# Retention recurrence on quarters of the TensorE array in 256-token steps, with a new order of the first steps

## The chip, the cores and the metric

The kernel runs on one core of a Trainium2 chip. The metric is the time of one execution on the device in microseconds (us). The kernel before takes 194.77 us, the median of three runs (194.75 to 195.33).

A core has a matrix engine, TensorE (PE in the profile; its weight loads, which overlap its matmuls, are PEld), and three others that are used here: VectorE (DVE), ScalarE (ACT) and GpSimd (POOL). SyncE's queue (SP) issues all DMAs. PE multiplies a stationary operand (`lhsT`, loaded as weights) with a moving one (`rhs`) and writes to PSUM, which has eight banks of 512 float32 a partition; DVE and ACT read PSUM, POOL only SBUF.

## What is computed

```python
gamma = 1.0 - 2.0 ** (-5.0 - np.arange(H))          # H = 8 heads, D = 64, S = 768, B = 4
for t in range(S):
    state = gamma * state + einsum('bhd,bhe->bhde', k[:, :, t], v[:, :, t])
    y[:, :, t] = scale * einsum('bhd,bhde->bhe', q[:, :, t], state)
x = y.transpose(0, 2, 1, 3).reshape(B * S, H * D)     # 3072 x 512
out = ((x @ w1) * (x @ w2)) @ w3 @ w_out              # 512 -> 1024 -> 1024 -> 512
```

The first half is a linear attention whose state (64 x 64 a head) decays by a factor of its head. The second is an FFN with a product of two projections. Inputs and output are float32; matmuls run in float16.

## The kernel before, in words

**Weights.** `w3 @ w_out` is multiplied out once: the rows of w3 are cast to float16 (`cast_w3`), transposed on PE (`w3_transpose`, lines 270 and 279), copied back (line 262) and multiplied with w_out (lines 291 and 304) to `W3O`. The FFN then has three products for each block of tokens: `a_unit` (w1) and `b_unit` (w2) through `mm`, line 537, eight blocks each, and `o_unit` (line 563) for each 128 tokens. ACT copies a's PSUM to SBUF (line 547), DVE multiplies b's PSUM into it (line 553), ACT scales and copies the output (line 568), and SP stores it (line 570).

**Recurrence.** It goes in chunks of 128 tokens, 24 in all, six to a sequence. For a chunk:

- `scores` (line 466): k times q, eight matmuls of 128x128x128. Two heads share the 128 partitions, so k is padded with zeros: `kp` holds the one head's k in partitions 0 to 63 and zeros below, and the other way round for the other head. DVE multiplies the result with the causal mask `keep` (line 471).
- `outputs`: v times the masked scores (lines 506 and 507; `vp` is padded in the same way) and, but for the first chunk of a sequence, the state times q (line 509). DVE scales with `YS` and writes x transposed, `xt` (line 514).
- `kv` (line 489): k times v. DVE adds the old state (line 497), POOL multiplies with the decay `GS`, whose zeros keep the two heads apart (line 498).

The decay within a chunk is in two exponentials, one multiplied into v (`VS`, POOL, line 383, which is also the cast of v), one into the output (`YS`). q and k are cast by POOL (lines 338 and 379) and transposed: in the first chunks on PE (lines 359, 400, 450), later by DMA (lines 420 and 424). ACT copies the transposed k into its padded place (lines 440 and 441).

**Order.** The Tile framework sets the semaphores, and each engine runs its instructions in program order. The opening is written out by hand (lines 674 to 812): w3 in column and row pieces as they land, chunks 0 to 3, and the FFN of the first 256 tokens by rows of the weights (`by_rows`, line 760). Then `step(n)` runs for each chunk (line 631): `fill` is a queue of FFN units with estimated costs, and `fill.pull` places them between scores, state and outputs, so that PE has work while DVE and POOL do theirs. `load_chunk(n + 4)` and `casts(n + 2)` run ahead.

Of the kernel before, what the change touches and what calls it, by code (L numbers as in the profile page):

```python
# [10 lines left out]
HP = mybir.dt.float16  # L11
AF = mybir.ActivationFunctionType
MULT = mybir.AluOpType.mult
ADD = mybir.AluOpType.add
PSUM = bass.MemoryType.PSUM
# [3 lines left out]
def kernel(  # L19
# [13 lines left out]
    C = 128  # L33
    WST = 12
    NCH = S // C
    NSTEP = B * NCH
    NTOK = B * S
    DT0 = 6
    NP = H // 2
    DM = 512  # L40
    DFF = 1024

# [5 lines left out]
    wstage = ctx.enter_context(tc.tile_pool(name="wstage", bufs=WST))  # L48
    xpool = ctx.enter_context(tc.tile_pool(name="xpool", bufs=4))
    ld = ctx.enter_context(tc.tile_pool(name="ld", bufs=6))  # L50
    att = ctx.enter_context(tc.tile_pool(name="att", bufs=2))
    fsb = ctx.enter_context(tc.tile_pool(name="fsb", bufs=2))

    ps_t = ctx.enter_context(tc.tile_pool(name="ps_t", bufs=1, space=PSUM))
    ps_at = ctx.enter_context(tc.tile_pool(name="ps_at", bufs=1, space=PSUM))
    ps_f = ctx.enter_context(tc.tile_pool(name="ps_f", bufs=3, space=PSUM))
# [4 lines left out]
    def dma_in(dst, src):  # L61
        nc.sync.dma_start(dst, src)  # L62

    chunk_in = {}
    q_in = {}
    pair_in = {}

    def load_pair(m, names="qkv"):

        b, c = divmod(2 * m, NCH)  # L70
        for nm, src in (("q", q), ("k", k), ("v", v)):
            if nm not in names:
                continue
            if nm == "q":
                t = ld.tile([128, 2 * 512], FP, tag="q64", name="q64", bufs=3)
                q_in[m] = t
            else:
                t = new_stage()
                pair_in[nm, m] = t
            dma_in(  # L80
                t[:, :].rearrange("p (h x) -> p h x", x=2 * D),
                src[b, :, c * C : (c + 2) * C, :].rearrange("h (p t) d -> p h (t d)", t=2),
            )

    def load_q4(half):

        t = ld.tile([128, 2 * 512], FP, tag="q64", name="q256", bufs=3)
        dma_in(
            t[:, :].rearrange("p (h x) -> p h x", x=4 * D),
            q[0, half * 4 : half * 4 + 4, 0 : 4 * C, :].rearrange("h (p t) d -> p h (t d)", t=4),  # L90
        )
        q_in["half", half] = t

    def load_chunk(n):
        if n >= NSTEP:
            return
        b, c = divmod(n, NCH)
        tiles = []
        if c % 2 == 0:

            t = ld.tile([128, 2 * 512], FP, tag="q64", name="q64", bufs=3)
            dma_in(
                t[:, :].rearrange("p (h x) -> p h x", x=2 * D),
                q[b, :, c * C : (c + 2) * C, :].rearrange("h (p t) d -> p h (t d)", t=2),
            )
            q_in[n // 2] = t
        for nm, src in (("k", k), ("v", v)):
            t = ld.tile([128, 512], FP, tag=nm + "32", name=nm + "32")
            dma_in(
                t[:, :].rearrange("p (h d) -> p h d", d=D),  # L110
                src[b, :, c * C : (c + 1) * C, :].rearrange("h i d -> i h d"),
            )
            tiles.append(t)
        chunk_in[n] = tiles

    def new_stage():
        return wstage.tile([128, 1024], FP, tag="wst", name="stg")

    def load_rows(src, i):
        t = new_stage()  # L120
        dma_in(t[:, :], src[i * 128 : (i + 1) * 128, :])
        return t

    def load_wo(i):

        t = new_stage()
        dma_in(
            t[:, :].rearrange("p (t n) -> p t n", t=2),
            moe_w_out[i * 256 : (i + 1) * 256, :].rearrange("(p t) n -> p t n", t=2),
        )  # L130
        return t

    def load_w3_columns(i):

        t = new_stage()
        dma_in(
            t[:, :].rearrange("p (f c) -> p f c", f=4),
            moe_w3[0:512, i * 256 : (i + 1) * 256].rearrange("(f p) c -> p f c", p=128),
        )
        return t  # L140

    w3c_st, wo_st = [], []
    for i in range(4):
        w3c_st.append(load_w3_columns(i))
        wo_st.append(load_wo(i))
    w3_st = {f: load_rows(moe_w3, f) for f in range(4, 8)}
    load_q4(0)
    load_q4(1)
    load_pair(0, "kv")
    w1_st = [load_rows(moe_w1, d) for d in range(4)]  # L150
    load_pair(1, "k")
    w2_st = [load_rows(moe_w2, 0)]
    load_pair(1, "v")
    w2_st += [load_rows(moe_w2, d) for d in range(1, 4)]
    for n in range(4, 8):
        load_chunk(n)
# [3 lines left out]
    KP = [const.tile([128, NP, 2, 128], HP, name=f"kp{i}") for i in range(2)]  # L160
    VP = [const.tile([128, NP, 2, 128], HP, name=f"vp{i}") for i in range(3)]

    def zero(t):
        nc.vector.memset(t[:, :, :, :].rearrange("p a b c -> p (a b c)").bitcast(FP), 0.0)

    zero(VP[0])
    ident16 = const.tile([128, 128], HP, name="ident16")
    make_identity(nc, ident16[:, :])


    ip_i = const.tile([128, H], mybir.dt.int32, name="ip_i")
    nc.gpsimd.iota(ip_i[:, :], pattern=[[0, H]], base=1, channel_multiplier=1)
    if_i = const.tile([128, 128], mybir.dt.int32, name="if_i")
    nc.gpsimd.iota(if_i[:, :], pattern=[[1, 2], [2, 64]], base=1, channel_multiplier=0)
    LGH = const.tile([128, H], FP, name="LGH")
    LGP = const.tile([128, NP], FP, name="LGP")
    for h in range(H):
        r = (h % 2) * 64
        nc.gpsimd.memset(LGH[:, h : h + 1], -math.log(gam[h]))
        nc.gpsimd.memset(LGP[r : r + 64, h // 2 : h // 2 + 1], math.log(gam[h]))  # L180

    keep = const.tile([128, 128], FP, name="keep")
    nc.gpsimd.memset(keep[:, :], 1.0)
    nc.gpsimd.affine_select(
        out=keep[:, :], in_=keep[:, :], compare_op=mybir.AluOpType.is_ge, fill=0.0,
        base=0, pattern=[[1, 2], [2, 64]], channel_multiplier=-1,
    )


    VS = const.tile([128, H], FP, name="VS")  # L190
    YS = const.tile([128, NP, 128], FP, name="YS")
    GS = const.tile([128, NP, 128], FP, name="GS")
    vs_x = const.tile([128, H], FP, name="vs_x")
    nc.vector.tensor_tensor(vs_x[:, :], ip_i[:, :], LGH[:, :], MULT)
    if_f = const.tile([128, 128], FP, name="if_f")
    nc.vector.tensor_copy(if_f[:, :], if_i[:, :])
    nc.scalar.activation(VS[:, :], vs_x[:, :], AF.Exp)
    for p in range(NP):
        nc.scalar.activation(YS[:, p, :], if_f[:, :], AF.Exp, scale=LGP[:, p : p + 1])

    keep2 = const.tile([128, 128], FP, name="keep2")
    nc.gpsimd.memset(keep2[:, :], 1.0)
    for t in range(2):
        r = slice(t * 64, t * 64 + 64)
        nc.gpsimd.affine_select(
            out=keep2[r, :], in_=keep2[r, :], compare_op=mybir.AluOpType.is_ge, fill=0.0,
            base=-t, pattern=[[1, 2], [2, 64]], channel_multiplier=-2,
        )

    ip2_i = const.tile([128, 2, H], mybir.dt.int32, name="ip2_i")  # L210
    for c in range(2):
        nc.gpsimd.iota(
            ip2_i[c * 64 : c * 64 + 64, :, :], pattern=[[1, 2], [0, H]], base=1, channel_multiplier=2
        )

    zero(KP[0])
    zero(KP[1])

    for i in (1, 2):
        nc.gpsimd.memset(VP[i][:, :, :, :].rearrange("p a b c -> p (a b c)").bitcast(FP), 0.0)  # L220
    nc.gpsimd.memset(GS[:, :, :], 0.0)
    for h in range(H):
        p, r = h // 2, (h % 2) * 64
        nc.gpsimd.memset(GS[r : r + 64, p, r : r + 64], gam[h] ** C)

    XT = {}


# [5 lines left out]
    W3h = {}  # L234
    w3t = {}

    def cast_to(dst, src, on_dve):
        if on_dve:
            nc.vector.tensor_copy(dst, src)  # L239
        else:  # L240
            nc.scalar.copy(dst, src)  # L241

    def cast_wo(i):
        cast_to(WO[i][:, :, :].rearrange("p a n -> p (a n)"), wo_st[i][:, :], i % 2 == 1)

    def cast_w3(key, st):
        t = att.tile([128, 1024], HP, tag="w3h", name="w3h", bufs=4)
        cast_to(t[:, :], st[:, :], False)
        W3h[key] = t
# [3 lines left out]
    def bank(tag, shape, dtype, name):  # L253
        return (ps_t if tag == "psT" else ps_at).tile(shape, dtype, tag=tag, name=name)

    def w3_bank(key, i):
        src, tag = W3h.pop(key), ("psA1", "psK")[i % 2]
        return src, ps_at.tile([128, 1024], HP, tag=tag, name="psW3")

    def w3_back(key, ps):  # L260
        t = att.tile([128, 1024], HP, tag="w3t", name="w3t", bufs=3)
        nc.vector.tensor_copy(t[:, :], ps[:, :])  # L262
        w3t[key] = t
# [601 lines left out]
```

## Time and profile before

| | before |
|---|---|
| median of three runs | 194.77 us |
| span of the profiled execution, first to last instruction | 193.1 us |
| what the timed runs have around the span | 1.7 us |
| first matmul starts, last one ends | 1.5 us, 190.1 us |
| PE busy | 184.1 us (95%) |
| DVE, ACT, POOL busy | 117.0, 103.3, 83.6 us |
| matmuls | 1785 |
| DMA | 40.5 MB, 84007 packets |

The profile is of one execution. "Busy" is the time in which an engine had an instruction in it; matmuls overlap, so a busy PE says only that it did not stand empty. "The chain that ended last" is followed back from the last instruction, at each step to what released it. Clock: PE was granted its full clock throughout.

### The profile page before, as it was taken

The numbers are of one execution on the slowest core, as the hardware profiler recorded it, in microseconds if no ns is written. First come the engines' busy times: TensorE is split into PE (matmuls) and PEld (weight loads), VectorE is DVE, ScalarE is ACT, GpSimd is POOL, SyncE is SP. The second block draws the span as 40 slices with busy tenths as digits, with TensorE's granted clock in tenths as the row PEclk, the third lists the DMA queues.
The fourth block names the chain that finished last, engine by engine and source line by source line (L and its number), as shares of the span: only waits on it lengthen the run. The fifth ranks groups of instructions, "written<-read, shape, count | busy, mean of one in ns | idle before, by whom it ended". The sixth has DMA issues, their size and how long they took to land.

```text
span 193.1 us, 4713 instructions
## 1 busy us (share of the span) xinstructions
PE 184.1 (95%) x1785; PEld 139.8 (72%) x1785; DVE 117.0 (61%) x220; ACT 103.3 (54%) x198; POOL 83.6 (43%) x144
## 2 busy tenths in 40 slices
PE   6698999979999999999999999999999999999993
PEld 2234557778797789777977797788777877887752
DVE  3225479699587758656665676565656665753220
ACT  6478598972454465354635463555355545533322
POOL 7600257728864737476252742863426432200000
PEclk9999999999999999999999999999999999999999
DMA  6999999998999999999999989969979930111104
GB/s 207 349 389 398 326 377 355 368 266 198 235 204 221 199 231 237 144 247 211 231 273 187 223 188 223 206 149 270 199 178 201 206 94 19 59 54 54 38 28 154
DMA packets 84007, 40.54 MB, mean 210 GB/s; under 512 B 61329, under 2 KB 78993, under 8 KB 83985
## 3 DMA queue, kind: packets, MB, share of 16 engines
q1 hardware_dynamic: 83984, 40.25, 88.5%
q8 instruction: 14, 0.23, 0.5%
q14 instruction: 9, 0.07, 0.2%
HBM read 29.36 MB, written 6.29 MB: 185 GB/s over the span
## 4 chain that ended last, share of the span: by engine, by line
PE 81%; DMA 10%; ACT 4%; DVE 2%; SPq 1%; issue 0%
PE psF L537 39%; PE psO L563 21%; DMA q<-in_q_dram 6%; PE psA L466 5%; DMA stg<-in_moe_w_out_dram 5%; PE psY L506 3%; PE psY L507 3%; PE psF L760 2%; PE psY L509 2%; PE psK L489 2%; SPq L62 1%; PE psG L537 1%; PE psO L580 1%; ACT w3o L241 1%; PE psG L760 1%; DVE vp L329 1%
## 5 line engine op out<-in xcount | busy, mean ns | idle before, releaser
L537 PE MATMUL psF<-xt,w 128*128 128x256 f16 (+1 forms) x736 | 85.0, 266 | 0.0
L537 PEld LDWEIGHTS <-w 128*128 128x128 f16 x768 | 68.2, 98 | 7.2
L553 DVE TENSOR_TENSOR ht<-pa,psF 128x256 f16<-128x256 f32 x88 | 36.6, 416 | 22.4 <-PE psF L537 13.1
L547 ACT COPY pa<-psF 128x256 f32<-128x256 f32 x84 | 31.3, 372 | 33.4 <-PE psF L537 33.0
L471 DVE TENSOR_TENSOR am<-psA,keep 128x512 f16<-128x512 f32 x48 | 30.9, 684 | 21.4 <-PE psA L466 21.3
L563 PE MATMUL psO<-w3o,ht 128*128 128x512 f16 x184 | 43.3, 379 | 0.0
L498 POOL TENSOR_TENSOR t<-s,GS 128x512 f16<-128x512 f32 x15 | 19.3, 1285 | 38.7 <-DVE s L497 38.7
L568 ACT ACTIVATE osb<-psO 128x512 f32<-128x512 f32 x23 | 13.7, 598 | 37.3 <-PE psO L563 37.3
L563 PEld LDWEIGHTS <-ht 128*128 128x128 f16 x184 | 17.8, 98 | 16.9 <-DVE ht L806 0.2
L383 POOL TENSOR_TENSOR vp<-v,VS 128x256 f16<-128x256 f32 x40 | 23.8, 617 | 6.9 <-DMA v<-in_v_dram 3.3
L514 DVE TENSOR_TENSOR xt<-psY,YS 128x512 f16<-128x512 f32 x24 | 17.8, 742 | 4.1 <-PE psY L509 3.8
L506 PE MATMUL psY<-am,vp 128*128 128x128 f16 x96 | 16.8, 219 | 0.9 <-POOL vp L329 0.7
L507 PE MATMUL psY<-am,vp 128*128 128x128 f16 x96 | 16.7, 219 | 0.6 <-DVE vp L329 0.6
L466 PEld LDWEIGHTS <-kp 128*128 128x128 f16 x192 | 12.5, 98 | 4.5 <-DVE kp L239 0.2
L338 POOL CAST q<-q 128x1024 f16<-128x1024 f32 x10 | 10.6, 1057 | 11.9 <-DMA q<-in_q_dram 11.9
L379 POOL CAST k<-k 128x512 f16<-128x512 f32 x20 | 12.3, 613 | 5.5 <-DMA v<-in_v_dram 2.4
L497 DVE TENSOR_TENSOR s<-psK,t 128x512 f32<-128x512 f32 x16 | 11.0, 688 | 2.8 <-PE psK L489 2.5
L262 DVE COPY w3t<-psW 128x1024 f16<-128x1024 f16 x8 | 5.5, 690 | 10.9 <-PE psW L270 8.5
L466 PE MATMUL psA<-qTd,kp 128*128 128x128 f16 x144 | 11.1, 219 | 0.0
L509 PE MATMUL psY<-qTd,t 128*128 128x128 f16 x60 | 10.8, 219 | 0.0
L440 ACT COPY kp<-kT 64x512 f16<-64x512 f16 x17 | 10.5, 618 | 0.4
L441 ACT COPY kp<-kT 64x512 f16<-64x512 f16 x17 | 10.5, 615 | 0.4
(87 smaller groups left out, 193.9 us busy)
## 6 DMA issues: line engine op xcount, KB each, us to landing
stg<-in_moe_w_dram SPq DMA_DIRECT2D x16, 512.0 KB, 8.5
q<-in_q_dram SPq DMA_DIRECT2D x12, 512.0 KB, 5.4
out_dram<-osb SPq DMA_DIRECT2D x23, 256.0 KB, 3.2
k<-in_k_dram SPq DMA_DIRECT2D x20, 256.0 KB, 5.3
v<-in_v_dram SPq DMA_DIRECT2D x20, 256.0 KB, 5.5
stg<-in_moe_w_out_dram SPq DMA_DIRECT2D x4, 512.0 KB, 8.2
stg<-in_k_dram SPq DMA_DIRECT2D x2, 512.0 KB, 9.9
stg<-in_v_dram SPq DMA_DIRECT2D x2, 512.0 KB, 9.7
```

The source lines that it names most:

```text
L383: nc.gpsimd.tensor_tensor(vp[:, :, r, r * 64 : r * 64 + 64], v32[:, :].rearrange("j (p s e) -> j p s e", s=2, e=64)[:, :, r, :], VS[:, :]. ...
L466: nc.tensor.matmul(ps[:, i, r, :], lhsT=kp[:, p, r, :], rhs=queries(n, p), start=True, stop=True)
L471: nc.vector.tensor_tensor(am[:, half * 2 : half * 2 + 2, :, :].rearrange("j p s i -> j (p s) i"), ps[:, :, :, :].rearrange("j p s i -> j ( ...
L498: eng.tensor_tensor(t16[:, :, :], s32[:, :, :], GS[:, :, :], MULT)
L506: nc.tensor.matmul(ps[:, p, :], lhsT=vp[:, p, 0, :], rhs=am[:, p, 0, :], start=True, stop=False)
L507: nc.tensor.matmul(ps[:, p, :], lhsT=vp[:, p, 1, :], rhs=am[:, p, 1, :], start=False, stop=(c == 0))
L509: nc.tensor.matmul(ps[:, p, :], lhsT=Tst[0][:, p, :], rhs=queries(n, p), start=False, stop=True)
L514: nc.vector.tensor_tensor(XT[n // 2][:, :, n % 2 * C : (n % 2 + 1) * C].rearrange("p a (i t) -> p a t i", t=2), ps[:, :, :].rearrange(orde ...
L537: nc.tensor.matmul(ps[:, i * w : (i + 1) * w], lhsT=W[d][:, (f + i) * 128 : (f + i + 1) * 128], rhs=XT[self.tok0 // TB][:, d, c0 : c0 + w] ...
L547: nc.scalar.copy(self.pa[f][:, :], ps[:, :])
L553: nc.vector.tensor_tensor(self.HT[:, f : f + TB // self.width, :].rearrange("p f n -> p (f n)"), self.pa.pop(f)[:, :], ps[:, :], MULT,)
L563: nc.tensor.matmul(psO[:, :], lhsT=self.HT[:, f, tb * 128 : (tb + 1) * 128], rhs=W3O[f][:, :], start=(f == 0), stop=(f == 7),)
```

## The change

The FFN and the product of w3 and w_out compute what they did, in the same matmuls. What is different:

- **Steps of 256 tokens** (`T`), 12 in all, three to a sequence, in place of chunks of 128. Loads, casts and transposes are by step.
- **Quarters.** Each matmul of the recurrence takes 64 partitions and gives 64: its `lhsT` and `rhs` lie in one half of the partitions, its result in one half, so that it stands on one quarter of the array. Nothing is padded with zeros any more: `KP`, `VP`, and ACT's copies into them are gone, as is the 128-wide `GS`. `QUARTERS` is the order in which the four are issued.
- **Chunks of 64 tokens from step 2 on** (`EO = 2`); steps 0 and 1 keep chunks of 128, with even and odd tokens in turn. Scores and av are then done for 64 x 64 blocks, and there are four states a step (`state`, three DVE sums and one that POOL decays).
- **`fence`**: ACT copies one column of each chunk from the PSUM of `inter` (state times q) to a tile that nothing reads, before `av` adds into the same PSUM.
- **Order.** A step's scores, k'v, masks and states are computed one step ahead, its casts three ahead and its transposes two. On PE each step is `inter(n)`, `scores(n + 1)`, `kv(n + 1)`, `av(n)`, the two output units of step n - 1, and the a- and b-units of step n, two blocks of 256 columns to a PSUM bank, so that ACT and DVE read 512 columns at a time. `fill` and its costs are gone.
- **The opening** is a new list: loads (w3 in rows alone, k of step 0 before the last of them, w1 and w2 by rows in another order), which engine casts what, and the place of every piece, until step 4. The warm-up has 8 matmuls of 512 columns, not 13.

The core of the diff follows: the quarters; the matmuls of scores from step 2 on, of k'v (`o` is `KB[n][g][half(r), t, a, :]` there), of `inter`, then `fence`, and `av`; the order of the loads; and the main loop (`LAST` is 3):

```diff
+    QUARTERS = ((0, 0), (1, 1), (0, 1), (1, 0))
+    def half(x):
+        return slice(x * 64, x * 64 + 64)
+    def qchunk(n, r, a, s, g):
+        c = 2 * s + g
+        return qT[n][half(r), :, a, c * 32 : (c + 1) * 32]
...
+            ps = [bank(t, [128, NP, 2, 64]) for t in tags]
+            for a in range(NP):
+                for s in range(2):
+                    for r, g in QUARTERS:
+                        nc.tensor.matmul(
+                            ps[r][half(g), a, s, :], lhsT=kT[n][half(r), s, a, half(g)],
+                            rhs=qchunk(n, r, a, s, g), start=True, stop=True,
+                        )
...
+                    nc.tensor.matmul(
+                        o, lhsT=k16[n][half(g), t, hd], rhs=v16[n][half(g), t, hd],
+                        start=(a == 0 and t == 0), stop=(t == 1), skip_group_check=True,
+                    )
...
+                        o, rhs = X[n, g][half(r), a, s * 64 : (s + 1) * 64], qchunk(n, r, a, s, g)
+                    nc.tensor.matmul(
+                        o, lhsT=TS[n, c][half(r), a, :], rhs=rhs, start=((g, r) not in begun), stop=False,
+                        skip_group_check=True,
+                    )
...
+    def fence(n):
+        for g in range(2):
+            if (g, 0) in X[n]:
+                s0 = 0 if n < EO or (n, (0, g)) in TS else 1
+                t = att.tile([128, NP, 2 - s0], FP, tag=f"fence{g}", name="fence")
+                nc.scalar.copy(t[:, :, :], X[n, g][:, :, :].rearrange("p a (s i) -> p a s i", s=2)[:, :, s0:, 0])
...
+                        o, rhs = X[n, g][half(r), a, t * 64 : (t + 1) * 64], am[n, None, r][half(g), a, t, :]
+                    nc.tensor.matmul(
+                        o, lhsT=v16[n][half(g), t, h * D : (h + 1) * D], rhs=rhs,
+                        start=((g, r) not in begun), stop=(n >= EO or t == 1), skip_group_check=True,
+                    )
...
+    fetch(
+        "r4 wo0 r1 r2 wo1 r5 wo2 r3 r6 k0 r7 wo3 q0 v0 r0 q1 k1 v1 w11 w13 w10 w12 w22 w23 w21 w20 "
+        "v2 v3 k2 q2 k3 v4 q4"
+    )
...
+    for n in range(LAST, NS):
+        nxt = n + 1 < NS
+        if n > LAST:
+            inter(n, ("X0", "X1"))
+            fence(n)
+            if nxt:
+                scores(n + 1, ("S0", "S1"))
+                kv(n + 1, ("K", "F1"))
+            av(n)
+            x_out(n, 0)
+            x_out(n, 1)
+            if nxt:
+                states(n + 1)
+                mask(n + 1, 0)
+                mask(n + 1, 1)
...
+            loads(n + 4)
+            casts(n + 3)
+            o_unit(n - 1, 0, ("F2",))
+            o_out(n - 1, 0)
+            o_unit(n - 1, 1, ("F0",))
+            o_out(n - 1, 1)
+        tags = ("F2", "F0", "F1")
+        for u in range(4):
+            a_unit(n, u, tags[2 * u % 3])
+            b_unit(n, u, tags[(2 * u + 1) % 3])
+            if n == LAST:
+                catch_up(u)
+        if n > LAST:
+            cast_queries(n + 3)
```

In the load list rN, woN, w1N and w2N are pieces of 512 KB of w3, w_out, w1 and w2, and kN, qN, vN are step N's. The list of the opening's pieces (some 190 lines) runs from the warm-up to the a- and b-blocks of steps 0 and 1, done by rows of w1 and w2 as these land, and to steps 2 and 3, whose recurrence is broken into shorter pieces between output units. In it `o_unit(0, 0)` is the first output unit.

## The prediction

> **What bounds the kernel now.** I read the page's engine table and slices first, then the chain that ended last, then one period of that chain, then the DMA share by stage.
>
> ```profile
> span 193.1 us, 4713 instructions
> ...
> PE 184.1 (95%) x1785; PEld 139.8 (72%) x1785; DVE 117.0 (61%) x220; ACT 103.3 (54%) x198; POOL 83.6 (43%) x144
> ...
> PE   6698999979999999999999999999999999999993
> ...
> PE 81%; DMA 10%; ACT 4%; DVE 2%; SPq 1%; issue 0%
> ```
>
> TensorE (PE) has no free slice from the middle of the span on, and the chain is PE for 81%; the DMA and ACT shares are the opening. The chain between 104.7 and 117.9 us holds one period of 256 tokens (start, length, what):
>
> ```profile
> 104.73 0.45 PE psA L466 x8
> 105.17 1.31 PE psF L537 x12
> 106.48 0.22 PE psK L489 x4
> ...
> 109.56 1.73 PE psO L563 x8
> ...
> 117.85 0.06 PE psA L466
> ```
>
> PE waits for nothing here. The paces are 0.45/8 = 56 ns for 128 columns, 1.31/12 = 109 ns for 256 and 1.73/8 = 216 ns for 512, so a matmul with its weight load costs its columns. The period is 117.85 - 104.73 = 13.12 us. The FFN takes 64 x 109 + 16 x 216 ns = 10.44 of it (lines 537 and 563). The recurrence takes the other 2.68: scores 2 x 0.45, state 2 x 0.22, outputs 2 x 12 x 56 ns = 1.34.
>
> By the groups of PE's instructions kept apart by shape, there are 820 matmuls of 128 columns, 688 of 256, 261 of 512, and 16 of the last output. At these paces (136 and 83 ns for the last 16, in proportion to their columns) that is 179.0 us. PE's last matmul ends at 190.1, so 11 us are lost, nearly all before 46.8 us, where the output matmuls of the first 256 tokens start. So two things can gain: fewer PE cycles in the recurrence, and a denser opening.
>
> **The recurrence, steps 2 to 11.** A step has 256 tokens. Its 48 matmuls of 128 columns become 128 of 64 columns, each on a quarter of the array: 32 scores, 32 k'v, 32 state-times-q, 32 av (some fewer in steps that begin or end a sequence). The trace has no matmul on a quarter, so I bound its cost by the 56 ns row:
>
> - Cheapest: four run side by side, each for 64 columns, so 28 ns a group of four. The state-times-q matmuls use only the two diagonal quarters, so 28 ns a pair. 24 x 28 + 16 x 28 ns = 1.12 us a step.
> - Dearest: side by side not at all, and the number of instructions counts as now: 128 x 56 ns = 7.2 us. If columns count, 128 x 28 ns = 3.6 us.
>
> I take a value near the cheap end, 28 to 50 ns a group (1.1 to 2.0 us): the row shows a cost that follows the columns, with no floor of its own down to 128, and the four quarters have different rows, columns and PSUM halves.
>
> Going from whole-array matmuls to quarters and back may cost the overlap that the pipeline has now. A 128-column matmul lasts 219 ns (line 466) and the next starts after 56, so between 0 and 163 ns a switch; I take 163. Two switches a step in the main loop: 0.33 us.
>
> The Trainium skill ("TensorEngine Tiling (Array Packing)", Key Properties) says the same of a change of tiling mode, that it drains the engine; no run here shows it yet. A rule that speaks against the change stands in "TensorE: Matmul & The Clock Gate" (Part 1): matmuls never start closer than about 25 ns, however few their columns. By that a step would be 128 x 25 ns + 0.33 = 3.5 us and the whole about 199.6; but its Part 3 has matmuls in different tiles of the array start some 4 ns apart. The trace, with nothing under 56 ns, decides neither.
>
> **A wait is added:** `fence`. ScalarE reads the PSUM of state-times-q before `av` may add to it, so `av` waits for ACT, and behind `av` on PE stand both output units. ACT's smallest rows are 216 ns (128x16) and 331 ns (128x192), so two fences are 0.43 to 0.66; I take 0.5. Ahead of them ACT has the copy of the last a-block (0.58, line 241's 128x512) and the q cast (1.05). From the end of that last a-block on PE: ACT is free at 0.2 + 0.58 + 1.05 = 1.83. PE does the b-block (0.87), drains (0.16) and does state-times-q (0.45 to 0.8), whose result is there at 1.65 to 2.0. Fences end at 2.35 to 2.5, and PE, which has scores and k'v of the next step as cover (0.45 to 0.8), starts `av` at 2.45 to 2.65, takes 0.22 to 0.4, and drains. The stretch is 1.97 to 2.35 us. **I take 2.1 us a step against 2.68.** Without cast and fence in the way it would be 1.12 + 0.33 = 1.45.
>
> The other engines have room in a step of 10.44 + 2.1 = 12.5 us. DVE: two x_out 0.74, four states 0.42, two masks 0.68, four b-blocks 0.68 = 7.2. ACT: four a-blocks 0.58, two output copies 0.60, q cast 1.05, fences 0.5 = 5.1 (the padding copies of lines 440 and 441, 21 us in all, go). POOL: k cast 1.05, v twice line 498's 1.29, last state 0.6 = 4.2. Masks, states, casts and transposes are all done a step ahead, under FFN matmuls; without that cover masks and states alone would cost 3 us a step.
>
> **DMA** carries the same bytes in the same packet sizes. Its share by stage (us, PE, PEld, DVE, ACT and POOL busy, PEclk, DMA share, GB/s):
>
> ```profile
> 20.00:30.00 10.00, 9.57 (x86) 5.79 (x84) 6.54 (x14) 7.85 (x14) 4.76 (x7) 1.00 1.11 355
> 117.85:130.97 13.12, 13.12 (x131) 10.51 (x129) 8.44 (x16) 6.64 (x14) 6.94 (x9) 1.00 0.95 200
> ```
>
> 0.95 x 13.12 = 12.5 us of DMA a step by its own share, which counts overlapping packets, so 12.5 is an upper end. A step of 12.5 us is just at it; that is the cover most easily lost. On SP each step issues two transposes, loads and two stores; the stores wait for ACT's output copies as now (line 570), with loads for four steps on ahead of them.
>
> **The opening.** The same 26 tiles of 512 KB (13.6 MB) must land before steps 0 and 1 can finish. The first eight slices (4.83 us each) move 207 + 349 + 389 + 398 + 326 + 377 + 355 + 368 GB/s = 13.4 MB, so the last tile of w2 lands near 39 us in any order. After it the list holds a cast (0.73) and 13 groups of four 256-column matmuls (13 x 0.436 = 5.7), so steps 0 and 1 finish their a- and b-blocks at about 46. PE's own work agrees: warm-up until 5.1 (now 13 matmuls, then 8), w3 times w_out 64 x 216 + 64 x 56 ns = 17.4, q and k transposes 1.8, recurrence of two steps 2.9 (32 groups of four and 12 pairs at 56 ns, 16 groups at 28), 14 switches 2.3, a- and b-blocks 14.0: 43.5 with no wait, and 2.5 us of waits in it is my choice. Engine queues in it: DVE takes the first w3 cast (0.73, line 239) that ACT does now (1.04 from 4.59 on), behind the exponents' arguments, which wait as now for POOL's sixteen small memsets (1.4 us); what is behind it is PE's first transpose (5.68 now), so this start can move by some 0.3 us either way. k of step 0 comes 10th, q and v 13th and 14th, all before the last rows of w3, so scores can fill the waits for w3; POOL's v casts (2.6 us each) are the longest pieces, and `av` is behind them. Now PE at 46.8 still owes the second 256 tokens 5.2 us of a and b (three quarters of 6.98), so it stands at 52.0 in the same count: 6 us gained.
>
> **The sum.** From 46: outputs 12 x 3.46 = 41.5; a- and b-blocks 10 x 6.98 = 69.8; stretches 10 x 2.1 = 21; transposes of step 2, 0.9; four more switches in steps 2 to 4, 0.7; a wait of 1.0 for k and q of step 2, which come 27th to 30th in the load order. PE ends at 180.9 against 190.1. The end stays (193.1 - 190.1 = 3.0): span 183.9. The timed runs lie 194.77 - 193.1 = 1.7 over the span: **185.6 us**.
>
> **Rivals.**
>
> 1. *Quarters don't run side by side; slower.* Price: 128 x 28 ns + 0.33 = 3.9 us a step, 18 over my sum in ten steps, and about 4 in the opening (7 more, part of it in waits for DMA): 207 us. At 56 ns each it would be over 240. The break-even is 9.2 us over my sum: 0.92 us a step, a stretch of 3.0, so about 21 ns a quarter matmul; above that the change loses. For it: PE now has no group in which two matmuls run at once. Against: cost follows columns.
> 2. *DMA takes over.* It has shares of 0.92 to 1.29 in every stage from 60 to 157 us at 13.1 us a step. If it needs 13 us a step (0.5 more than mine, over eight steps), 4 us are lost: 190. For it: shares over 1. Against: it runs ahead now, and its share is 0.17 from 157 us on, 36 us before the end.
> 3. *Fence and casts cost nothing, and quarters run at the cheap end:* 10 x 0.65 less, and the opening at 43.5: 176.6.
> 4. *The opening's order fails:* a hand-made order on five engines, where one late tile holds a whole queue. Its 6 us go: 191.6; with 3 us of waits more, no gain.
>
> **Chances.** Forecast (180 to 189) 0.45; fully side by side (175 to 180) 0.15; DMA (189 to 193) 0.11; opening 0.10 (half of it at or over 194); no side by side 0.19. The bands are times in us. Within 0.3% of 194.77 is about what the measurement can tell from no change (0.6 us): 0.04, from the edges of the opening and DMA cases. Faster: 0.45 + 0.15 + 0.11 and 0.03 of the opening's, 0.74; slower 0.22. The range, 175 to 200, leaves out most of rival 1 and little else.
>
> **What would show it.** Chain: stretches of quarter matmuls of 2.1 us with 10.44 between; 3.5 or more is rival 1. Waits: PE for ACT's fence, 0.3 to 0.6 us a step. DMA-bound: PE or POOL waiting for k or v, or PE for a transpose. Opening: the first output matmuls near 46 us. The forecast is wrong if quarters cost over 21 ns each, or if PE has gaps of over 1 us between 20 and 60 us.

## The result, and the profile after

| | before | after |
|---|---|---|
| median (lowest to highest), 4 runs each | 194.88 us (194.75 to 195.33) | 192.73 us (191.95 to 193.91) |
| ratio, 95% interval | | 0.989 [0.985, 0.993] |
| predicted | | 185.6 us (175 to 200) |
| profiled execution, its span | 194.77, 193.1 us | 193.91, 192.2 us |
| last matmul ends | 190.1 us | 189.2 us (predicted 180.9) |
| matmuls | 1785 | 2592 |

The change is 1.1% faster, with an interval clear of 1: the forecast sign, a quarter of the forecast size (2.1 us of 9.2). Ratios leave out runs in which the core was disturbed, the profiled ones of e2 and e8 below among them, so they need not equal the quotient of the medians. The profiled execution is the slowest of the four; what follows of waits and terms is read from it.

From the page of the changed kernel, the lines that answer to those of before:

```profile
span 192.2 us, 5984 instructions
...
PE 175.9 (92%) x2592; PEld 125.7 (65%) x2592; DVE 100.1 (52%) x171; ACT 71.1 (37%) x131; POOL 50.9 (27%) x79
...
PE   7489999999999794998888979999999999999993
...
PEclk9969999999999999699999999999999999999999
...
PE 41%; DMA 5%; ACT 0%; issue 0%
```

PE's work fell by 8 us and its span by 1: between 62 and 115 us it now has slices that it doesn't fill (slices 14 to 24, 4.8 us each), where before it had none, and two slices are below full clock. The chain can be followed back only to 101.4 us, so its 41% are most of the 91 us from there to the end; DMA, which came in at the opening alone, now stands in it twice, at 109.8 and 145.7 us, each time with a transpose of q.

The chain of waits in a period that nothing disturbs (start, length, what; k'v lies between 126.53 and 126.81):

```profile
118.66 7.01 PE psF L482 x64
125.66 0.56 PE psX L423 x28
...
126.28 0.25 PE psS L333 x27
...
126.81 0.28 PE psX L448 x32
127.09 3.56 PE psF L530 x16
130.65 1.44 PE psF L482 x13
```

The a- and b-blocks and the outputs cost what they did (7.01 + 3.56 = 10.57). The stretch of state-times-q, scores, k'v and av is 127.09 - 125.66 = **1.43 us**, against 2.68 before and 2.1 predicted; the period is 130.65 - 118.66 = 11.99 us, against 13.12.

Where the 8 us went shows in the timeline (start, length, engine and line, operation, tiles, and in brackets the idle time before it and what ended it). `st` is the buffer in which a load lands, `ht` DVE's product of a and b, `osb` ACT's copy of an output. From four queries on 55 to 77 us:

```profile
55.76 1.34 SPq L293 DMA_TRANSPOSE kT<-k  x1
57.19 1.50 SPq L80 DMA_DIRECT2D st<-in_q_dram  x1
58.79 1.86 SPq L85 DMA_DIRECT2D st<-in_k_dram  x2
...
65.95 0.69 DVE L58 CAST k<-st 128x1024 f16<-128x1024 f32 x1 [4.96 <-DMA st<-in_k_dram]
66.56 1.28 DVE L61 TENSOR_TENSOR ht<-pa,psS 128x512 f16<-128x512 f32 x2
67.30 1.03 PE L482 MATMUL psS<-xt,w 128*128 128x256 f16 x8 [1.32 <-DVE ht L61]
67.58 1.29 SPq L293 DMA_TRANSPOSE kT<-k  x1
68.91 0.71 SPq L80 DMA_DIRECT2D st<-in_q_dram  x1
...
75.04 1.04 ACT L58 CAST q<-st 128x1024 f16<-128x1024 f32 x1 [2.99 <-DMA st<-in_q_dram]
75.99 0.59 ACT L541 ACTIVATE osb<-psF 128x512 f32<-128x512 f32 x1
76.63 1.77 PE L482 MATMUL psF<-xt,w 128*128 128x256 f16 x11 [2.75 <-ACT osb L541]
```

Read it upwards from the last line. PE waits 2.75 us for a PSUM bank. ACT frees it (`osb`), but ACT stood 2.99 us in front of the cast of q of step 5, whose load had not landed. That load was issued at 68.91, because SP held it behind the transpose of k of step 4, and this waited for a cast on DVE, which waited 4.96 us for its own load. DVE's wait held the `ht` behind it, and so cost PE 1.3 us at 67.3. At 91.9 us the same happens on ACT, at 101.4 with the fence behind a late q cast, and at 114.1 PE waits for a transpose itself:

```profile
91.91 1.25 PE L482 MATMUL psF<-xt,w 128*128 128x256 f16 x10 [1.49 <-ACT osb L541]
...
101.43 0.51 PE L448 MATMUL psX<-am,v 64*64 64x64 f16 x32 [1.20 <-ACT fence L436]
...
114.10 0.45 PE L333 MATMUL psS<-qT,kT 64*64 64x64 f16 x32 [1.12 <-DMA qT<-q]
```

A wait is counted here from the time at which the next matmul could have started, about 0.16 us before the modelled end of the last one, so each is 0.16 us more than its bracket. So counted, PE's waits of over 0.25 us between 60 and 117 us add up to **8.7 us** (the five brackets to 7.9); after 117 us only one is left (0.44 at 174.7).

The longest wait also costs clock. By the windows, the granted clock is 0.5 at 77.4 to 80.85 us, right behind it, and at 9.17 to 12.58 us, behind a wait of 1.7; each time 3.41 us, or 1.7 us of matmuls lost. Before, no half clock is recorded between 5.5 us, where the record begins, and the end (the first warm-up matmuls, 427 ns for 512 columns, ran at half pace). The clock isn't the whole loss: the fastest run of after, 191.95 us, had a mean clock of 1.0.

### The profile page after: what moved, and what is told of

It is laid out like the page before. It is cut to its first block, busy times and chain, and to the rows that moved or that the text cites. A ratio compares the mean times of both kernels' runs of the same rounds, so it can differ in the third digit from the quotient of the medians.

```text
span 192.2 us, 5984 instructions
## 1 busy us (share of the span) xinstructions
PE 175.9 (92%) x2592; PEld 125.7 (65%) x2592; DVE 100.1 (52%) x171; ACT 71.1 (37%) x131; POOL 50.9 (27%) x79
## 3 DMA queue, kind: packets, MB, share of 16 engines
q1 hardware_dynamic: 83728, 40.38, 86.2%
## 5 line engine op out<-in xcount | busy, mean ns | idle before, releaser
L482 PE MATMUL psF<-xt,w 128*128 128x256 f16 x576 | 66.1, 276 | 4.2 <-ACT osb L541 4.2
L61 DVE TENSOR_TENSOR ht<-pa,psF 128x512 f16<-128x512 f32 x39 | 26.8, 687 | 43.1 <-PE psF L482 43.1
L530 PE MATMUL psF<-w3o,ht 128*128 128x512 f16 (+2 forms) x176 | 38.3, 370 | 0.0
L58 ACT COPY pa<-psF 128x512 f32<-128x512 f32 x39 | 22.8, 586 | 41.6 <-PE psF L482 36.5
L61 POOL TENSOR_TENSOR v<-st,VN 128x1024 f16<-128x1024 f32 x8 | 15.2, 1903 | 34.7 <-DMA st<-in_v_dram 34.7
L541 ACT ACTIVATE osb<-psF 128x512 f32<-128x512 f32 (+2 forms) x22 | 12.6, 576 | 29.0 <-PE psF L530 26.6
L465 DVE TENSOR_TENSOR xt<-psX,YN 128x512 f16<-128x512 f32 x18 | 12.2, 724 | 10.0 <-PE psX L448 10.0
L58 POOL CAST k<-st 128x1024 f16<-128x1024 f32 x8 | 8.3, 1038 | 17.7 <-DMA st<-in_k_dram 10.4
L58 ACT CAST q<-st 128x1024 f16<-128x1024 f32 x8 | 8.4, 1046 | 11.5 <-DMA st<-in_q_dram 11.5
L350 DVE TENSOR_TENSOR am<-psS,keep 128x512 f16<-128x512 f32 x15 | 9.6, 680 | 1.1 <-PE psX L333 1.1
L512 PE MATMUL psF<-xt,w 128*128 128x256 f16 x56 | 9.7, 273 | 0.0
```

The source lines that it names most:

```text
L58: {"v": nc.vector.tensor_copy, "g": nc.gpsimd.tensor_copy, "s": nc.scalar.copy}[eng](dst, src)
L61: (nc.vector if eng == "v" else nc.gpsimd).tensor_tensor(dst, a, b, op)
L350: nc.vector.tensor_tensor(t[:, :, :, :].rearrange("p a s i -> p (a s) i"), ps[:, :, :, :].rearrange("p a s i -> p (a s) i"), keep64[:, :]. ...
L465: nc.vector.tensor_tensor(XT[n][:, :, :].rearrange("p a (s x) -> p (a s) x", s=2)[:, :, g * 64 : (g + 1) * 64].rearrange("p k (i t) -> p k ...
L482: nc.tensor.matmul(ps[:, i, :], lhsT=W[d][:, f * 128 : (f + 1) * 128], rhs=XT[n][:, d, :], start=(i == 0 and d == 0), stop=(i == 1 and d = ...
L512: nc.tensor.matmul(rows_ps[w, n, uh][j // 2][:, j % 2, :], lhsT=W[d][:, f * 128 : (f + 1) * 128], rhs=XT[n][:, d, :], start=(first and j % ...
```

## The experiments

All medians stand beside the kernel before on the same chip (194.84 to 194.89). "Waits" are PE's of over 0.25 us between 60 and 117 us, "half clock" is the time at 0.5 after 40 us, both in the profiled execution.

| kernel | median us | ratio, 95% | waits us | half clock us |
|---|---|---|---|---|
| after | 192.73 | 0.989 [0.985, 0.993] | 8.7 | 3.4 |
| e1 narrow stores | 189.97 | 0.974 [0.969, 0.980] | 5.8 | 0 |
| e2 casts to POOL | 194.59 | 0.996 [0.993, 1.000] | 11.6 | 3.4 |
| e3 constants later | 191.70 | 0.984 [0.982, 0.985] | 8.0 | 0 |
| e4 one quarter in a row | 195.43 | 1.003 [1.000, 1.005] | 5.7 | 0 |
| e5 before, narrow stores | 194.74 | 1.000 [0.998, 1.001] | | |
| e6 more warm-up | 192.13 | 0.986 [0.982, 0.990] | 7.3 | 3.4 |
| e7 four q by PE | 191.73 | 0.979 [0.972, 0.985] | 4.2 | 3.4 |
| e8 big packets | 188.88 | 0.960 [0.951, 0.968] | 5.7 | 0 |
| e9 loads first | 200.96 | 1.027 [1.022, 1.032] | 13.3 | 17.1 |
| e10 = e9 + e8 | 195.11 | 1.000 [0.997, 1.004] | 9.3 | 10.2 |
| e11 = e9 + e7 + e6 | 203.61 | 1.041 [1.036, 1.047] | 12.7 | 13.7 |
| e12 steps 3 to 6 by PE | 190.36 | 0.979 [0.975, 0.984] | 2.2 | 0 |
| e13 = e12 + e8 | 190.78 | 0.979 [0.973, 0.984] | 2.2 | 0 |
| e14 = e12 + e6 | 190.72 | 0.978 [0.975, 0.981] | 2.2 | 0 |

Of the times that the expectations gave, only those of e3, e5, e6 and e13 came true, and but for e5 not for the reason given.

The theory was that DMA comes too late. The question behind it was which part of the way: the amount of DMA work; the order of the casts on DVE and ACT, which stand ahead of what PE needs; the order on SP, where loads wait behind transposes; or the transposes themselves, which go through the same queue as the loads.

**e1_narrow_stores**: less DMA work in the main loop.

```diff
         r0 = n * T + tb * 128
+        if n < 10:
+            c1 = c0 + 64
         nc.sync.dma_start(out[r0 : r0 + 128, c0:c1], o_sb[n, tb][:, c0:c1])
```

> The changed kernel, but of the outputs of steps 0 to 9 only the first 64 of 512 columns are stored (the rest of the output is left unwritten); every instruction and its order stay. A packet of 2 KB takes 86 ns and one of 256 B 18 ns in the trace of before, so a step's 256 store packets take 256 x 68 ns / 16 = 1.09 us less of the 16 DMA engines. Theory D (the sum of DMA work is late from 50 to 115 us, five steps): loads come up to 5 us earlier there, the waits of 8.7 us between 60 and 115 us and the half clock after the longest one shrink by half or more: 187 to 189 us. Theory O (an in-order engine is held by a cast that stands ahead of what PE needs; how much DMA work there is matters little): the waits stay for the most part: 191 to 193.

189.97 us: 2.8 less than after, yet waits of 5.8 us stay: between the two ranges expected. The amount has a part; a cut of some 1.1 us a step can't say how large a one.

**e5_before_narrow**: the same cut in the kernel before (`out[r0 : r0 + 128, 0:w]` with 64 columns on line 570).

> The kernel before with the same cut of the stores as in e1_narrow_stores (first 64 of 512 columns, up to token 2560). Its PE had no wait after 47 us, so theory D, by which DMA limits the changed kernel only because that asks for its data sooner, expects no change: 194.0 to 195.0. If less DMA work speeds PE in another way (ports, memory): about 2 us faster, as in e1.

No effect (0.998 to 1.001). DMA had slack before, so the lateness belongs to the change.

**e2_pool_casts**: the late casts leave DVE and ACT. The cast of q from step 5 on goes from ACT to POOL, that of k of steps 4 and 5 and of v of step 5 from DVE to POOL.

```diff
-    cast("k", 4, "v")
+    cast("k", 4, "g")
...
-    cast("q", 5, "s")
+    cast("q", 5, "g")
...
-            cast("q", n, "s")
+            cast("q", n, "g")
```

> The changed kernel with the casts that wait for late loads moved to POOL, which is busy for 27% of the span: all q casts from step 5 on (ACT before), k of steps 4 and 5 and v of step 5 (DVE before). Theory O: ACT's fences and output copies and DVE's b-blocks are no longer behind a cast, so the waits at 67, 77, 92 and 101 us (1.5 + 2.9 + 1.7 + 1.4) go, and with the second the half clock: 184 to 187 us. Theory D: PE then waits for the transposes of the same late q and k instead: 191 to 193, waits moved from ACT and DVE to DMA.

Slower than after, if by little (the two intervals touch), with 11.6 us of waits. PE's main wait in it (who waits for whom, us in total, times, longest):

```profile
PE psS L333 <- DMA qT<-q: 8.5, 3, 3.7
```

In after ACT's `osb` headed this list with 4.2 us. The casts in front of the evacuations were only where the lateness came out; cleared away, PE waits for the transposed q itself. The theory of the casts' order falls.

**e9_early_loads**: on SP each load goes ahead of the transposes that it stood behind.

```diff
-    fetch("q3 k4")
+    fetch("q5 k5 v5")
...
+    loads(6)
     dma_turn("k", 4)
-    fetch("q5 k5 v5")
...
-                turns(n + 2)
-                load("q", n + 3)
-                load("v", n + 3)
-            else:
-                turns(n + 2)
             loads(n + 4)
+            turns(n + 2)
```

> The changed kernel with another order on SP alone: from step 3 on each load stands ahead of the DMA transposes (which wait for a cast) in place of behind them, and q of step 3 before v and q of step 4. Theory S (new: SP's order holds the loads of steps 3 to 6 behind transposes that wait for casts that wait for loads, so DMA stands idle now and then while it is late): the waits between 60 and 115 us shrink by half or more: 187 to 190 us. Theory D (the amount of DMA work alone): the queues were full anyway, transposes come later by as much as loads come earlier: 192 to 195.

8.2 us slower than after. The transposes of q that SP issues at 62.57 in after start here at

```profile
69.18 3.07 SPq L293 DMA_TRANSPOSE qT<-q  x2
```

and PE waits 6.1 us once for a qT and 4.4 once for a kT. So the order on SP is no fault that can be turned round: loads put ahead of the transposes delayed these two by 6.6 us.

**e8_big_packets**: k and v of steps 3 to 11 are replaced by rows of w3 of the same size, which come in packets of 4 KB.

```diff
+        elif n > 2:
+            i = (2 * n + (nm == "v")) % 8
+            nc.sync.dma_start(t[:, :], moe_w3[i * 128 : (i + 1) * 128, :])
```

> The changed kernel, but k and v of steps 3 to 11 are read from rows of w3 in packets of 4 KB (other data, as many bytes) in place of 256 B packets; so the recurrence gets wrong k and v. By the packet times of the trace of before (18 ns for 256 B, 160 ns for 4 KB) a step's k and v take (4096 x 18 - 256 x 160) / 16 = 2.05 us less of the DMA engines. Casts, transposes, PE, ACT and DVE do the same. Theory D (DMA work is late from 50 to 115 us): nearly all 8.7 us of waits between 60 and 115 us and the half clock there go: 182.5 to 185 us. If something else than the amount of DMA work makes those waits: 190 or more.

188.88 us, with a wide spread (185.6 to 190.4). 48,906 packets in place of 83,754. In the profiled run (189.44) the waits after 100 us are gone, those between 68 and 92 us stay (5.7 in all): with 42% fewer packets the way of steps 3 to 6 was still late there. Transposes of k also landed later, a median of 6.1 us after their issue against 4.4 in after. What waits the fastest run, 185.59, had isn't recorded. By the medians e8 is 3.9 us faster than after, the largest gain of all: amount counts.

**e10_early_big** (e9 and e8 together):

> Both: the loads early as in e9_early_loads and k and v of steps 3 to 11 in 4 KB packets from w3 as in e8_big_packets (wrong k and v). With e8 alone the waits after 100 us went and those of 68 to 92 us (5.7 us) stayed. If amount and order together are the cause: no wait over 0.5 us after 47 us: 181 to 184. If a third cause holds PE between 60 and 92 us: as e8, 186 to 189.

195.11 us: with cheap packets the order of e9 still loses against e8 by 6 us.

**e7_pe_q**: q of steps 5 to 8 is transposed by PE and copied back by DVE, not by DMA (`if n not in BY_PE` ahead of the DMA, `turn("q", n, "X1")` and `turned("q", n, "v")` behind the outputs).

> The changed kernel with q of steps 5 to 8 transposed on PE (as q of steps 0 to 2 is) and copied back by DVE, not by DMA; the output is the same. Four transposes of 256 KB leave the DMA queues in the late stretch; PE gets 4 x 0.45 us more. Theory D: the transposes are only some of the DMA work, but q is there some 4 us (its time to landing) after its cast sooner, so the waits at 101 and 114 us go and those before shrink: 188 to 190.5. If the waits are set by the casts' place alone: 192.5 to 194.5, since PE has more to do.

191.73 us, between the two ranges. Waits are halved to 4.2; the two at 67.8 and 76.7 us, behind the transposes of k, stay.

**e11_early_pe_warm** (e9, e7 and e6):

> A version to use, with the right output: e9_early_loads with q of steps 5 to 8 transposed on PE (e7_pe_q) and the 13 warm-up matmuls of e6_warm. If amount and order are the causes, the three add up in part: 186 to 189. If the queues are full whatever the order: 190 to 192, as e7.

The worst of all, 203.61 us. k still goes by DMA here, behind the loads; PE waits 5.7 us once for a qT and 5.0 once for a kT.

**e12_pe_3_to_6**: k and q of steps 3 to 6 are transposed by PE, and the order is otherwise that of after. The main loop's part:

```diff
-            dma_turn("k", n)
-            dma_turn("q", n)
+            if n > 6:
+                dma_turn("k", n)
+                dma_turn("q", n)
...
+    def pe_turn(n, tag):
+        if n <= 6:
+            turn("k", n, tag)
+            turned("k", n, "v")
+            turn("q", n, "X1")
+            turned("q", n, "v")
```

> The changed kernel with k and q of steps 3 to 6 transposed on PE in place of DMA (banks that are free there, copied back by DVE); the output is the same. On SP the loads of steps 3 to 7 then follow each other with no transpose between them that waits for a cast, and 2 MB of transposes leave the queues; PE gets 8 x 0.45 = 3.6 us more, DVE 8 x 0.69. Theory T (new: it is the way of a step's q and k, load 6 us, cast, transpose 4 to 6 us in the same queues, that is late, not the amount or the order by itself): the waits of 8.7 us between 60 and 115 us fall under 2.5 and the half clock there goes: 186 to 188.5 us. Theory D (amount): waits fall by the 8 transposes' share, some 3 us, which PE's extra 3.6 take: 191.5 to 193.5.

190.36 us: the waits as theory T had them, the time between its range and D's. The windows (us; PE, PEld, DVE, ACT, POOL busy with instructions; clock; DMA share; GB/s), after first:

```profile
60.00:80.00 20.00, 15.88 (x251) 11.66 (x250) 10.95 (x20) 6.48 (x13) 2.45 (x3) 0.94 1.08 233
80.00:100.00 20.00, 18.51 (x338) 14.59 (x338) 9.40 (x16) 6.37 (x12) 3.92 (x3) 0.98 1.10 211
```

and the same of e12:

```profile
60.00:80.00 20.00, 18.25 (x306) 14.28 (x304) 15.79 (x26) 5.85 (x12) 3.93 (x4) 1.00 0.80 197
80.00:100.00 20.00, 20.00 (x389) 15.57 (x388) 11.44 (x19) 7.23 (x15) 4.84 (x3) 1.00 1.20 243
```

Waits fall from 8.7 to 2.2 us, the clock stays full, and from 80 to 100 us PE is never empty, at a DMA share of 1.20, more than in after. The 64 added matmuls cost 64 x 56 ns = 3.6 us of PE. 6.5 of waits and 1.7 of clock less 3.6 is 4.6; the spans differ by 192.2 - 187.5 = 4.7. These are the slowest run of after and the fastest of e12; by the medians the gain is 2.4 us. Three things changed at once, and no run parts them: the transposes, and what waits behind them on SP, are out of the way; there is less DMA work (8,448 packets, and in 60 to 80 us the share falls by 0.28, against 0.09 in e8, which spared 34,848 packets over nine steps and kept 5.7 us of waits); and PE, with 3.6 us more to do, asks later, which alone takes waits away, as e4 shows below. SP's own time to issue is a fourth candidate, since from 60 to 120 us its DMA instructions fill 92 to 95% of the time in after; against it, they fill only 51% from 60 to 80 us in e8, where waits stay.

**e13_pe_big** (e12 with the packets of e8):

> e12_pe_3_to_6 with k and v of steps 3 to 11 in 4 KB packets from w3 as in e8_big_packets (wrong k and v). If the amount of DMA work and the way through the transposes are the whole cause, no wait over 0.5 us is left after 47 us but the last step's: 185 to 187 (181.5 to 183.5 and PE's 3.6). If PE is held by something else: waits of over 3 us stay, 189 or more.

```profile
60.00:80.00 20.00, 18.25 (x303) 13.98 (x302) 15.64 (x28) 5.89 (x11) 2.90 (x3) 1.00 0.48 167
```

The DMA share goes from 0.80 to 0.48 and PE is busy for the same 18.25 us, with the same waits. Once the transposes of these steps are off the queue, a further cut of the amount changes nothing here. (This profiled run's opening was slower: its first output unit starts at 50.1.)

**The quarters themselves: e4_one_quarter.** Scores and av are issued quarter by quarter, so that matmuls in a row stand on the same one.

```diff
-            for a in range(NP):
-                for s in range(2):
-                    for r, g in QUARTERS:
+            for r, g in QUARTERS:
+                for a in range(NP):
+                    for s in range(2):
```

> The changed kernel from step 2 on with scores and av issued quarter by quarter (eight matmuls in a row on one quarter) in place of four quarters in turn; the same 64 matmuls a step. If the four run side by side only because neighbours in the order are on different quarters (28 to 32 ns a group of four in the trace), eight in a row take 28 ns each: 64 x 28 = 1.8 us for the two against 0.6 now, 1.2 us a step, ten steps: 12 us in all, less what DMA waits hide (up to 5): 199 to 205 us. If the order is of no matter: 192 to 193.

The same period in its chain:

```profile
117.97 7.01 PE psF L487 x64
124.98 0.62 PE psX L423 x32
125.60 0.61 PE psS L333 x29
...
126.47 0.71 PE psX L453 x32
```

Scores take 0.61 us and av 0.71, against 0.25 and 0.28: 0.8 us a step, so some 8 us in ten steps. The first matmuls of a quarter start 32 ns apart. That the 32 of av take 0.71 and not 32 x 32 ns = 1.02 us is because the next quarter's first ones start beside the last of the quarter ahead, even before them: at 126.03 three matmuls of k'v start ahead of three scores, at 126.06 to 126.12, that precede them in the program. So the 12 us expected were too many. And the kernel is only 2.7 us slower than after: waits fall by 3.0 and the half clock's 1.7 goes. Over half of what PE loses, DMA's lateness gives back, as it took the gain before.

**The opening: e3_opening** moves the late constants (`step_decays`, `late_numbers`, `late_arguments`, `late_tables`) behind the w3 casts.

> The changed kernel with the constants that are first used in steps 0 (state decay) and 2 (the 64-token exponentials and mask) moved from the first 10 us to where ACT, DVE and POOL have room, after the casts of w3. PE loses 3.7 us in waits before 12 us now and then has half the clock from 9.2 to 12.6 us. Both theories: the gap of 1.7 us before the second w3 transposes goes, the clock stays up, and steps 0 and 1 are through about 3 us earlier. Theory D: the loads of step 2 and later come no earlier, so the gain is given back as waits between 45 and 115 us: 191.5 to 193 us. Theory O: a part is kept: 189 to 191.

191.70 us, but not by the opening: the waits of its first 10 us stay at 3.1, and the first output unit starts at 49.81, 1.0 later than in after. The profiled run lacks the half clock of 77 us.

**e6_warm**: 13 more warm-up matmuls of 512 columns between the first w3 blocks.

> The changed kernel with 13 more warm-up matmuls (5, 5 and 3 of 512 columns) in the waits of the first 11 us, where PE has its first transposes and the kernel before had 5 such matmuls. If the half clock from 9.2 to 12.6 us (to 14.5 in some runs) comes from the waits before it, the clock stays up and the first output unit starts at 46.5 to 47.5 us (48.8 now). Theory D: half or more of these 1.5 to 2 us is given back as waits between 60 and 115 us: 191 to 192.5. If the opening alone counts: 190 to 191.

The clock stays full from 6.9 to 68 us, and the waits of the first 10 us shrink to 0.26; the 13 matmuls fill them, PE waits 0.9 us at 26.8 instead, and the first output unit starts at 48.70, where it was (48.79). **e14_pe_warm** repeats it on e12:

> A version to use: e12_pe_3_to_6 with the 13 warm-up matmuls of e6_warm. By theory T, 185 to 187.5 us; by theory D as e12, 191 to 193.

No gain either (190.72 against 190.36; first output at 50.25). And in e12 itself matmuls of 128 columns start 107 ns apart, half pace, up to 13.4 us, yet its first output, at 48.50, is the earliest of all these. By these runs the clock of the opening costs nothing that shows in the first output.

## Why the prediction was right or wrong

Against its sum, for PE's last matmul (180.9 predicted, 189.2 measured):

| term | predicted | measured | difference |
|---|---|---|---|
| opening up to the outputs | 46.0 | 49.2 (first unit at 48.79, with 0.43 of step 1 still owed) | +3.2 |
| waits in steps 2 to 6 | 1.0 | 8.7 | +7.7 |
| half clock behind them | 0 | 1.7 | +1.7 |
| ten stretches | 21 | 14.3 (1.43 each) | -6.7 |
| outputs and blocks, 12 x 3.56 + 10 x 7.01 | 111.3 | 112.8 | +1.5 |
| last wait | 0 | 0.44 | +0.4 |

Together +7.8 of 8.3; the transposes of step 2 and the four further switches, 1.6 in the sum, weren't measured by themselves. The amount of DMA work is, as predicted, no more than before: the queue's packets took 88.5% of 16 engines' span before and 86.2% after.

- **The quarters: right, and mis-sized to the safe side.** Side by side was right and rival 1 is refuted: matmuls on the four quarters start 2 to 4 ns apart, and a group of four takes about 32 ns, of the 28 to 50 allowed; what was over was the wait for the fence. The switch was priced at 163 ns; into the quarters the first start is 203 ns behind a 256-column matmul's instead of 109, and out of them 125 instead of about 28: 0.1 us each.
- **The fence: right that it may cost, wrong where.** It was to set the stretch at 2.0 to 2.35. In undisturbed periods PE doesn't wait for it (1.43 is the figure that the prediction gave "without cast and fence in the way", 1.45); it costs only behind a late q cast (1.2 us at 101.4), 0.2 at 29.4 in the opening, and in the last step.
- **"a wait of 1.0 for k and q of step 2": the step that failed.** The term stood for all lateness of DMA. The prediction took the bytes of the opening up to w2 and the share of a step in the main loop, and nothing of what lies between: from 49 us on PE asks for each step's k and q a step ahead, while their loads come last in the order and each goes load, cast, transpose, with transposes and loads in one queue. It cost 8.7 us, and 1.7 of clock. Rival 2, DMA at 190, was nearest in its mechanism (rival 4's 191.6 is nearer as a number, but the opening lost 3.2 us only), and its sign (PE for a transpose) was seen; but it put the loss in the amount of work of eight steps. The prediction's own alarm, gaps of over 1 us between 20 and 60 us, looked at the wrong stretch: PE's are between 67 and 115. That DMA is late for the faster PE is shown: less DMA work helps (e1, e8) and did nothing before (e5). e8 and e1 show that amount has a part. In e12 the waits nearly go with the transposes of steps 3 to 6 off the queue, and a share of 1.20 stands beside a PE that never waits; how much of that is the way through the queue, how much the amount and how much PE's later demand stays open.
- **The opening: half right.** "2.5 us of waits in it is my choice" was too little. The order gained 52.0 - 49.2 = 2.8 of the 6. e3, e6 and e14 moved waits and clock about and left the first output at 48.7 to 50.3; that the arrival of the 26 tiles sets it is argued, not shown.
- **DVE, ACT and POOL have room: right** (52, 37 and 27% busy); their waits were for DMA.
- **No sign that the change fails to do what it says.** Its gain is there: 12.5 us in ten stretches and 2.8 in the opening. Of these 15.3, waits and clock took 8.7 + 1.7 + 0.4 = 10.8 back. The last matmul ends only 0.9 us earlier: 1.5 more went to outputs and blocks, and some 2 us, the transposes of step 2 and switches among them, aren't traced.

A rule of the Trainium skill spoke against the change ("TensorE: Matmul & The Clock Gate", Part 1: starts never closer than about 25 ns). The trace: e4's 32 ns on one quarter is above that; 2 to 4 ns between different quarters is below it, and agrees with that page's Part 3 (some 4 ns a tile). So the rule holds here for a quarter, not for the engine. The same page (Part 1) has the clock halved after at least one idle window of about 3.4 us. The windows at 0.5 last 3.41 us in after, but the waits ahead of them were 1.7 (with one of 1.3 shortly before) and 2.9 us, shorter than one window.

**Open:** which part of DMA's way is late, as said at e12; the 2.2 us of waits left in e12 (0.95 of it for DVE's copy of a transposed k at 72.8); what sets the first output; and what makes runs of one kernel differ by 2 us, with mean clocks of 0.97 to 1.0. e12 has the lowest median of the kernels that do the whole work, but its interval overlaps those of e7 and e14.

## What to carry to other kernels

When an edit makes the bounding engine faster, its demand moves forward in time: draw up for the first steps when each input is asked for and follow its whole way back, load, cast, transpose, with every queue that it shares; a mean share of DMA says neither yes nor no. A late load is seen first on the evacuations that stand behind its cast, and here moving the cast only moved the wait. Taking transposes off the loads' queue for the steps right after the opening paid here (2.4 us by the medians), even at 3.6 us of the bounding engine.

## What the runs showed of the hardware

- Four 64x64x64 matmuls with weights of their own, one on each quarter, take about 32 ns together; in a row on one quarter 32 ns each. Changing between whole array and quarters costs 0.1 us.
- Behind waits of PE the clock fell to 0.5 for 3.41 us, or two or three times that. The length of one wait doesn't tell: 2.75 us of idle time (after, to 76.6) and 1.2 and 0.6 close together (e6, to 68.3) were followed by it, 3.1 (e2, to 85.3) and 2.35 (e3, to 76.5) were not. In after the two stretches start 68.27 us apart, 20 times 3.413, so the count may go by fixed stretches of that length, which a wait can straddle; no run here tests it.
- A DMA transpose of k lands a median of 4.4 us after its issue in after and 5.6 in e9, with the same sizes and only the order changed (one of q 4.3 and 3.9).
